# Another order of the 766 steps of a hand-scheduled attention and expert kernel

## Chip, core and metric

The kernel runs on one NeuronCore of a Trainium2 chip, as one launch. The metric is the device time of a launch in microseconds (us). The profile names the core's engines PE (TensorE, matmuls), PEld (its weight loads, which overlap matmuls), DVE (VectorE), ACT (ScalarE), POOL (GpSimd) and SP (SyncE, which here only issues transfers). PSUM, into which TensorE writes, has 8 banks of 128 x 512 float32.

## The reference

Two stages, with batch 4, sequence 768. The first is attention of 8 heads of 64 columns, in which each row sees its neighbours closer than 16 and one summary key and value of each of the 24 blocks of 32 rows. The second takes the 512 columns of the 8 heads as `x`, and runs 4 experts of causal attention with a head of 64, of which a gate picks 2 per row.

```python
k_sum = k.reshape(B, H, nb, block, D).max(axis=3)      # nb = 24, block = 32
v_sum = v.reshape(B, H, nb, block, D).mean(axis=3)
scores_l = scale * q @ k^T, masked to |i - j| < 16
scores_s = scale * q @ k_sum^T + log(block)
attn = softmax([scores_l, scores_s]) @ [v, v_sum]
...
logits = x @ w_gate                                     # 2 of 4 experts per row
for e in range(E):
    q, k, v = x @ wq[e], x @ wk[e], x @ wv[e]
    ye = softmax(causal(scale * q @ k^T)) @ v @ wo[e]
    out += w[e] * ye                                    # where e was picked
```

## The kernel before

The kernel has no scheduler at run time or at build time: `make_plan` lists 766 steps, each a few instructions with the buffers that it reads and writes, and `TABLE` (lines 55 to 108) is a text of 766 entries `step,engine,slots` that says in which order the steps are emitted, on which engine each runs (V VectorE, A ScalarE, G GpSimd, S SyncE, P TensorE), and which slots its new buffers take. `Plan.emit` walks the table; a semaphore is waited for wherever a step reads what another engine wrote, or overwrites a slot that another engine still reads. Each engine takes its own entries strictly in the table's order, so a step that waits holds up all later steps of its engine, transfers that this engine issues among them.

Steps have names. `b` is the batch (0 to 3), `c` the pair of heads (0 to 3), `g` the half of the heads, `cc` the pair of experts, `u` a block of scores (0 to 5):

- loads: `dk`, `dq` (keys and queries, issued by GpSimd, lines 261 and 266), `dv` b c (values, four transfers from SyncE into one of six `vb` slots, lines 284 to 287), `dw..`, `dwo`, `dwg` (weights), `dvs` (values by blocks of 32 into the one `vt` slot, line 339);
- set-up: `id16`, `id32`, `idr` (identities), `mt` (mask), `pi`, `kwz`, `knz` (three memsets of 4 x 1024 into the key slots, line 219), `sel` (the selector of block sums, lines 240 to 244), `vtz`, `v2o`, `vone` (ones in a `vb` slot, lines 210 to 214), `w1m` and `at` (a first exponential), `cvg`, `cg`, `cw0`, `cw1`, `co` (weights to half precision);
- block sums: for batches 0 and 1 by TensorE, `bs` (line 304), then `be` on VectorE (L170, L322) and `ds`, a copy into the `vb` slot; for batches 2 and 3 by GpSimd, `tr` (line 347) and `ds`. `hc` copies 32 rows of each window within the `vb` slot (L170, 32 x 1408);
- first stage, per b and c: `tk`, `tq` (transposes, L366), `kw`, `rk`, `ksc`, `cq` (key windows, block maxima and queries out of PSUM, and the copy of the key sums, L170, 128 x 288), `sc` (scores, L414 and L420), `ex` (exponentials, L427), `av` (L437), `rc`, `xm` (division, L448 and L452), `tx` (transposes, L463), `hi`, `lo` (two half-precision parts, L482);
- second stage, per b: `vp` (values and gate, L554 and L557), `lg`, `v2`, `ga`, `gx`, `gb`, `gc` (gate); per cc: `pp` and `pc` (projections, L630, and their copy to half precision), `sp` (scores, L654), `es` (exponentials, L662), `dm` (causal mask, L667, on GpSimd), `aw` (L678), `r2`, `wv` (L697 to L704), `tw` (L715), `ct`; then `op` (L737), `oc` (copy out of PSUM) and `od` (transfer to memory, L748);
- `fl0` to `fl23`: dummy matmuls on zeros (L769), four of 512 columns for the first eight and one for the others. With engine P they run; with engine A the entry emits nothing.

The digits behind a name are b, c or cc, and so on: `bs01` is the block sum of batch 0, pair 1; `pp310` a projection of batch 3, second pair of experts; `op34` the last piece of the output product. Lines such as L170 and L168 belong to a copy helper for all engines.

TensorE's array is used in different shapes: whole for `vp`, `pp`, `aw`, `op` and `fl`, in 64 rows for `sc`, `sp`, `tx`, `tw`, in 64 or 32 columns for `tk`, `tq`, `av`, `bs`.

Of the kernel before, what the change touches and what calls it, by code (L numbers as in the profile page):

```python
# [15 lines left out]
S = 768  # L16
# [42 lines left out]
95,A, 99,P,6.0.0 40,V,3 77,P,4.3 51,G, 234,S,3 68,P,0.0 78,A, 126,P,1.2 69,V, 80,A, 98,P, 243,G,0 127,A, 44,G, 70,A,  # L59
62,G, 122,P,4.2.2 236,S,4 100,V, 105,P,5.1.1 101,V, 82,P,2.1.1 148,G, 106,A, 81,P, 124,V, 102,P,0.0.0 83,V, 123,A,  # L60
125,G, 107,V, 109,P,6.0 233,G,2 103,A, 84,V, 45,G, 130,P,4.4 144,S,0 110,A, 104,V, 143,S, 269,P,7.0.0 131,A, 141,S,
235,G, 128,P,2.5 271,V, 63,P,6.1 129,A, 145,S,1 108,G, 133,P,0.0.2 270,A, 64,V, 140,S, 132,P, 142,S, 252,P,4.2.2
134,V, 111,P,2.0 135,V, 242,G,0 65,G, 254,V, 113,P,6.1 112,A, 237,G, 85,P,0.1.1 114,A, 86,V, 136,P,2.2.2 272,G, 137,A,
115,P,6.1.0 273,P,5.1 138,V, 150,G, 116,P, 274,A, 87,V, 46,V, 253,A, 238,P,2.0 117,V, 118,V, 246,S,5 277,P,0.2 239,V,
275,P,4.3 278,A, 119,P,6.3.3 256,P,3.2 276,A, 120,V, 241,G, 286,P,2.1.1 303,P,0.0.0 257,A, 194,P,4.0 121,V, 406,S,0
304,A, 244,S,2 255,G, 288,V, 149,G, 196,P,6.1 195,A, 305,V, 240,G, 287,A, 260,P,4.4 147,V, 407,S, 280,P,0.0.1 261,A,
409,S, 247,G, 290,P,3.0 197,A, 307,P,2.1 291,V, 279,P, 308,A, 204,P,4.0 402,S,4 281,V, 213,P,6 152,P,2.0.0 205,A,
282,V, 214,A, 245,G, 258,P,0.5 154,V, 283,P,4.4.4 259,A, 153,V, 408,S, 198,P,6 215,G, 201,P,2 284,V, 146,S, 199,A,
289,G, 248,P,0.1 418,S,0 306,G, 285,V, 401,G,1 202,A, 309,P,6.0 249,V, 210,P,4 310,A, 262,P,2.1.2 211,A, 263,P, 251,G,
165,P,0.2 250,A, 404,S,3 264,V, 265,V, 415,G,0 294,P,6.1 403,G, 166,A, 266,P,4.5.5 292,P,2.2 295,A, 267,V, 158,P,0  # L70
293,A, 400,G,0 151,A, 155,P,6 410,G, 159,V, 268,V, 160,A, 311,P,2.3 157,V, 207,P,4 312,A, 167,P,0.0 156,V, 161,V,6.0
208,A, 163,V, 411,G,0 314,P,2.0.0 162,A, 168,V, 432,P,7.2 313,P, 164,V, 433,A, 169,P,4.1 315,V, 172,P,0 170,A, 316,V,
413,G, 296,P,6.1.1 584,S,0 582,S, 585,S, 449,P,2.0 583,S, 173,A, 181,P,4 203,G, 450,V, 297,P, 412,G, 182,A, 184,P,0
178,P,2 416,S,2 298,V, 299,V, 185,A, 175,P,4 179,A, 209,G, 317,P,0.6.6 183,G, 300,P,6.7.7 174,G, 318,V, 176,A, 206,G,
428,P,2.2.2 200,G, 445,P,3.1.1 171,G, 319,V, 301,A, 177,G, 362,P,4.1 429,A, 414,G,2 447,V, 186,G, 180,G, 302,V,
364,P,0.0 448,A, 576,G,1 446,A, 430,V, 212,G, 586,G, 217,P,0.0.6 363,A, 218,P, 365,V, 431,A, 216,P, 375,P,2.0 219,V,
369,P,4 376,A, 187,P,1.1.0 220,V, 189,P, 587,G,1 370,A, 188,P, 434,P,2.5 190,V, 366,P,6 191,V, 323,P,4.1.1 367,A,
435,A, 436,P,0.4 417,G, 325,V, 420,S,0 453,P,6.3 423,S, 192,P,2.0 324,V, 454,A, 421,S, 320,P,4 193,V, 422,S, 368,G,
437,A, 578,S,5 405,G, 221,P,2.1 322,A, 372,P,6 222,V, 479,P,0.0.0 373,A, 419,G, 462,P,1.2.1 321,V, 381,P,2 223,P,4.0
464,V, 480,A, 577,G,2 335,P,6.2 382,A, 224,V, 463,A, 377,G, 383,G, 590,G,2 326,P,2 336,A, 481,V, 225,S, 371,G, 374,G,  # L80
378,P,4 327,V, 333,P,6.0 328,A, 329,V,1.1 424,G, 331,V, 330,A, 379,A, 229,P,2.2 332,V, 334,A, 451,P,4.0 230,V, 380,G,
226,P,0.4 452,A, 425,G,0 346,P,6.1 227,V, 343,P,4 347,A, 385,P,1.0.2 384,P, 386,P, 344,A, 228,S, 349,P,0 387,V,
# [819 lines left out]
```

## Time and profile before

| | us |
|---|---|
| median of 3 runs | 162.57 |
| lowest, highest | 161.71, 163.44 |
| profiled execution, its own time | 163.03 |
| its span (first to last instruction) | 161.3 |
| bytes read, written in it | 24.13 MB, 6.29 MB |

A profile is one execution of the program, recorded instruction by instruction. The span is shorter than the time by what lies before and behind. Busy time is the union of an engine's records; matmul records overlap, and each goes on some 0.2 us behind the point at which the next may start, so a short wait of TensorE can look shorter than it is. "Idle before" names what ended an idle stretch, read from the semaphores.

### The profile page before, as it was taken

What the parts mean: (1) busy time and instruction counts of PE and PEld (TensorE: products, weight loads), DVE (VectorE), ACT (ScalarE), POOL (GpSimd) and SP (SyncE); (2) the same over time, 40 slices, a digit from 0 to 9 for tenths busy, and PEclk for the clock granted to TensorE, in tenths of its full rate; (3) what the DMA queues carried; (4) which work ended last, traced back from release to release, by engine and by line L of the source; (5) the groups of instructions that cost most, each with busy time, mean ns of one, the idle gap of its engine ahead of it and who ended that gap; (6) DMA issues with size and microseconds to landing.
All of it is one profiled execution on the core that took longest, in us unless ns stands there. A gap on an engine that the chain in (4) does not pass through costs nothing.

```text
span 161.3 us, 6957 instructions
## 1 busy us (share of the span) xinstructions
PE 146.8 (91%) x2999; PEld 108.0 (67%) x2999; DVE 116.6 (72%) x241; ACT 117.9 (73%) x150; POOL 111.8 (69%) x181
## 2 busy tenths in 40 slices
PE   0249998899999999999999999999999998999997
PEld 0127796786776866688656979666778895476742
DVE  5675488989885577986877887847978578247770
ACT  3032499758998969988978795787867894999540
POOL 6899969777775999969999999629994340135100
DMA  3999999998699995993899749886000000030746
GB/s 27 210 220 212 205 179 227 209 219 163 154 176 207 228 207 135 171 201 53 201 219 221 216 107 161 191 291 254 24 0 4 4 4 0 6 130 0 257 167 230
DMA packets 44158, 24.57 MB, mean 152 GB/s; under 512 B 33120, under 2 KB 40544, under 8 KB 43744
## 3 DMA queue, kind: packets, MB, share of 16 engines
q1 hardware_dynamic: 35280, 16.52, 43.2%
q0 software_dynamic: 7488, 6.29, 26.2%
q10 hardware_dynamic: 1360, 1.32, 2.3%
q8 instruction: 23, 0.38, 1.0%
q14 instruction: 7, 0.06, 0.1%
HBM read 24.13 MB, written 6.29 MB: 189 GB/s over the span
## 4 chain that ended last, share of the span: by engine, by line
PE 65%; POOL 21%; issue 6%; ACT 4%; DVE 3%; POOLq 0%; DVEq 0%; ACTq 0%
PE ps L437 12%; PE ps L630 11%; POOL vb L170 7%; PE ps L554 6%; PE ps L678 6%; PE ps L304 4%; PE ps L366 4%; PE ps L654 4%; PE ps L737 3%; PE ps L463 3%; PE ps L414 3%; POOL vt L347 3%; PE ps L769 3%; POOL a L667 2%; PE ps L420 2%
## 5 line engine op out<-in xcount | busy, mean ns | idle before, releaser
L662 ACT ACTIVATE a<-ps 128x1024 f16<-128x1024 f32 (+1 forms) x48 | 41.8, 918 | 5.2 <-PE ps L654 4.8
L667 POOL TENSOR_SCALAR_AFFINE_SELECT a<-a 128x256 f16<-128x256 f16 x48 | 18.6, 406 | 21.0 <-ACT a L662 20.4
L427 ACT ACTIVATE aT<-ps 120x768 f32<-120x768 f32 x32 | 25.0, 816 | 9.2 <-PE ps L420 9.0
L437 PE MATMUL ps<-vb,aT 120*64 120x65 f32 x768 | 27.3, 224 | 1.2 <-issue 0.6
L437 PEld LDWEIGHTS ps<-vb,aT 120*64 120x64 f32 x768 | 24.4, 138 | 4.3 <-issue 2.1
L170 POOL COPY vb<-vb 32x1408 f32<-32x1408 f32 x16 | 21.9, 1373 | 2.9 <-DMA vb<-in_v_dram 2.1
L630 PE MATMUL ps<-hi,wqk 128*128 128x384 f16 x128 | 23.1, 326 | 0.7 <-ACT ob L168 0.3
L347 POOL TENSOR_TENSOR vt<-vt 120x1024 f32<-120x1024 f32 (+3 forms) x16 | 19.2, 1200 | 6.4 <-issue 4.1
L630 PEld LDWEIGHTS <-wqk 128*128 128x128 f16 x128 | 11.8, 98 | 9.6 <-issue 2.2
L382 DVE TENSOR_REDUCE ks<-ps 128x24 f16<-128x768 f16 x16 | 15.1, 951 | 3.7 <-PE ps L366 3.3
L482 DVE TENSOR_TENSOR lo<-ps,hi 128x768 f16<-128x768 f32 x16 | 15.1, 954 | 1.3 <-ACT hi L168 1.1
L452 DVE TENSOR_TENSOR x<-ps,rec 128x768 f32<-128x768 f32 x16 | 15.3, 956 | 0.5
L366 PE MATMUL ps<-idr,kn 100*64 100x100 f16 x256 | 8.5, 218 | 7.3 <-DMA kn<-in_k_dram 7.3
L654 PE MATMUL ps<-qk,qk 64*128 64x512 f16 (+3 forms) x128 | 14.4, 306 | 0.5 <-ACT qk L168 0.4
L554 PE MATMUL ps<-wvg,hi 128*128 128x264 f16 x96 | 13.8, 275 | 0.1
L170 POOL COPY vb<-vu 24x768 f32<-24x768 f32 x16 | 13.2, 822 | 0.8
L168 ACT COPY kw<-ps 128x1152 f16<-128x1152 f16 x12 | 13.5, 1133 | 0.0
L168 ACT COPY qT<-ps 128x768 f16<-128x768 f16 x12 | 9.5, 806 | 5.3 <-PE ps L366 5.2
L678 PE MATMUL ps<-v,a 128*128 128x65 f16 x336 | 12.3, 193 | 0.2
L366 PEld LDWEIGHTS <-kn 100*64 100x64 f16 x256 | 7.0, 116 | 8.1 <-DVE vb L210 5.7
L678 PEld LDWEIGHTS <-a 128*128 128x128 f16 x336 | 11.0, 97 | 2.1 <-issue 1.0
L737 PE MATMUL ps<-wo,wT 128*128 128x512 f16 (+1 forms) x50 | 11.9, 371 | 0.0
(95 smaller groups left out, 273.8 us busy)
## 6 DMA issues: line engine op xcount, KB each, us to landing
vb<-in_v_dram SPq DMA_DIRECT2D x32, 176.0 KB, 6.1
out_dram<-ob SPq DMA_DIRECT2D x9, 512.0 KB, 3.4
vt<-in_v_dram SPq DMA_DIRECT2D x16, 192.0 KB
kn<-in_k_dram POOLq DMA_DIRECT2D x6, 384.0 KB, 7.5
qn<-in_q_dram POOLq DMA_DIRECT2D x6, 384.0 KB, 7.4
out_dram<-ob ACTq DMA_DIRECT2D x2, 512.0 KB
kn<-in_k_dram POOLq DMA_DIRECT2D x4, 192.0 KB, 5.5
qn<-in_q_dram POOLq DMA_DIRECT2D x4, 192.0 KB, 5.5
```

Of the source, the lines that this page charges most:

```text
L168: nc.scalar.copy(dst, src)
L170: en(e).tensor_copy(dst, src)
L347: en(e).tensor_tensor(y[0:120], x[0:120, 0:w], x[0:120, w:2 * w], AL.add)
L366: nc.tensor.transpose(dst[64 * hp:64 * hp + 64, p * s:p * s + p], src[:, hh + hp, 64 * s:64 * s + 64], idt)
L427: nc.scalar.activation(T["aT"][aT.slot][0:KR], pbank(sc, 2)[0:KR, :, 0:384], AF.Exp, scale=SCALE)
L437: nc.tensor.matmul(pbank(av, 2)[o:o + 64, u, 65 * (2 * (t // 2) + hp):65 * (2 * (t // 2) + hp) + 65], a[0:KR, hp, 64 * t:64 * t + 64], T[" ...
L554: nc.tensor.matmul(p[:, i, 0:264], hi_(ch)[:, cols], T["wvg"][:, ch, :], start=(ch == 0), stop=False, skip_group_check=True)
L630: nc.tensor.matmul(pbank(pp, 2)[:, u, 0:384], T["wqk"][:, cc, ch, j, :], hi_(ch)[:, 384 * u:384 * u + 384], start=(ch == 0), stop=(ch == N ...
L654: nc.tensor.matmul(pbank(sp, 2)[:, ep, c0:c0 + w], T["qk"][qk[1].slot][r, 128 * tj:128 * tj + 128], T["qk"][qk[0].slot][r, n0:n0 + w], sta ...
L662: nc.scalar.activation(a2v(u), pbank(sp, 2)[:, :, 0:ln], AF.Exp, scale=SCALE / (XS * XS))
L667: nc.gpsimd.affine_select(m, m, [[0, 2], [1, 128]], AL.is_ge, 0.0, base=0, channel_multiplier=-1)
L678: nc.tensor.matmul(pbank(av, 2)[:, ep, 65 * ti:65 * ti + 65], a2v(u)[:, ep, o:o + 128], T["v2"][v2.slot][:, tj, 2 * cc + ep, :], start=(tj ...
```

## The change

The diff touches nothing but `TABLE`. All 766 steps, their instructions and their buffers are the same; the order, the slots, and the engine of 73 steps differ. The first three and the last three lines of the two tables:

```diff
-2,G,0 139,A, 41,V,4 6,G, 8,V, 52,S,4 4,G, 7,G, 37,G,0 42,V,5 0,G, 5,G,0 47,S,0 1,A, 36,G, 3,G, 39,V,2 66,S,2 35,G,
-34,V, 59,G,1 58,G,1 71,P,0.0.0 43,G, 88,P,1.1.1 53,G, 90,V, 61,S,5 60,G, 54,P,2.0 72,V, 91,A, 89,A, 48,G, 73,V,
-92,P,3.0 55,V, 57,G, 75,P,4.1 93,A, 232,G,0 49,P,5.1 76,V, 74,A, 56,G, 96,P,6.0 50,V, 94,P,0.1 97,A, 79,P,2.2 67,G,
...
-742,P, 746,V, 754,P,4.4 747,V, 714,V, 748,V, 751,P,6.2 755,A, 715,V, 749,P,2 23,P,0 752,V, 756,A, 716,P,4 31,P,1
-717,A, 32,P,0 17,A,1 30,P,1 750,V, 753,A, 757,P,4.6 763,P,5.0 758,A, 760,P,0.1 27,P,1 764,V, 21,P,6 11,A,7 26,A,2
-761,V, 25,A,3 19,P,2 759,S, 765,A, 13,P,7 762,A, 15,A,4 28,A,1 16,A,3 18,A,5 14,P,6 33,P,2 10,P,0
+40,V,3 4,G,0 39,V,2 52,S,3 2,G, 6,G, 5,G,0 139,A, 3,G, 7,V, 35,G, 57,G,1 8,G, 47,S,2 59,G, 53,A, 71,P,0.0.0 42,V,5
+37,V,0 88,P,1.1.1 34,V, 43,G, 66,S,5 58,G,1 73,V, 36,G, 54,P,2.0 90,V, 0,V, 75,P,3.0 74,A, 89,A, 92,P,4.1 41,V,4
+61,S,4 93,A, 48,G, 60,G, 91,G, 49,P,5.1 72,V, 55,V, 94,P,6.0 76,A, 56,A, 95,A, 96,P,0.1 232,G,2 67,G, 77,P,2.2 50,V,
...
+15,A,2 714,V, 575,S, 751,P,6.0 715,V, 716,P,2 717,V, 747,V, 754,P,0.4 748,V, 752,A, 17,A,2 749,P,2 19,A,6 32,P,6
+753,A, 755,V, 750,A, 757,P,7.6 760,P,6.2 26,P,4 763,P,5.3 761,A, 11,P,4 13,P,2 758,V, 31,A,3 764,V, 27,P,0 756,S,
+24,A,1 18,A,7 10,P,1 765,S, 16,P,6 759,A, 762,A, 28,A,5 21,P,4 30,P,5 20,A,7 23,A,7 14,A,7 25,P,7
```

Read by engine, with names, the parts that the text below speaks of:

```
GpSimd before  dk000 id16 dk001 idr vone0 w1m dq001 mt dq000 kwz dk011 dq010 sel hc01 dq011 hc00
               dk010 dk100 ds01 hc03 ds00 dq110 id32 hc02 cg ksc03 dq100 vtz hc10 ksc02 dk110 ds02
               hc11 ksc11 cw1 ds11 ksc10 cw0 ds10 hc13 hc12 dm015 ksc12 ksc13 dq200 ds13 ...
GpSimd after   dk001 dk000 id16 dq001 dq000 kwz dk010 knz dk011 sel dq010 mt hc00 dq011 ksc01 dk100
               hc03 ds00 dq110 hc02 id32 vtz dq100 ds03 ksc02 dk110 ds02 ksc10 hc11 cw1 hc23 ds10
               ds11 ksc13 co cvg hc13 hc12 cg cw0 dq200 v2o ds12 ...
SyncE before   dv01 dv00 dv03 dv02 dv10 dv11 dw11 dw10 dw01 dwv1 dw00 dwv0 dv13 dvs200 dv12 dvs201
               dvs203 dv20 dvs202 dwo dv23 ...
SyncE after    dv01 dv00 dv03 dv02 dv10 dv11 dw10 dw11 dv23 dv13 dwo dwv0 dwv1 dv12 dvs200 dw01 dw00
               dvs203 dvs201 dvs202 dv30 dv20 ...
TensorE before tk00 tk01 bs01 tq01 tq00 bs00 sc011 sc010 sc001 av011 sc000 bs03 tq03 av010 tk03 ...
TensorE after  tk00 tk01 bs01 tq00 tq01 bs00 sc010 sc011 sc000 tk03 bs03 sc001 tk02 av011 av010 ...
TensorE before ... op22 aw300 aw301 sp311 aw311 aw310 fl19 tw300 aw302 tw310 aw312 op31 op30 tw311
(its end)      fl13 tw301 fl21 fl22 fl20 op32 op34 op33 fl17 fl11 fl9 fl3 fl4 fl23 fl0
TensorE after  ... sp311 aw301 aw300 op21 aw310 aw311 op22 tw300 aw302 tw310 aw312 op30 tw301 op31
(its end)      tw311 fl22 op32 op33 fl16 op34 fl1 fl3 fl17 fl0 fl6 fl11 fl20 fl15
```

Of the 73 steps that change their engine, these go from GpSimd to ACT: `hc01`, `ds01`, `ksc03`, `hc10`, `ksc12`, `ds13`, `ksc22`, `ksc30` to `ksc33`; from ACT to GpSimd: `ksc01`, `ds03`, `ds12`, `co`, `ksc20`, `ksc21`; from DVE to GpSimd: `knz`, `v2o`, `cvg`; from GpSimd to DVE: `idr`, `vone0`, `w1m`, `ksc11`. 18 copies out of PSUM go from DVE to ACT and 18 others from ACT to DVE; three output transfers change between ACT's and SyncE's queues. The dummy matmuls that run number 22 instead of 21.

More of the change, by code (lines that the diff above doesn't have):

```diff
@@ L61 @@
[L61 to L70, printed above, removed]
@@ new lines @@
+142,S, 145,S, 117,V, 244,S,4 273,P,1.0 235,A, 238,P,6.0 137,A, 256,P,7.2 274,A, 406,S,0 118,V, 270,A, 138,V, 257,A,
+119,P,2.3.3 141,S, 150,G, 275,P,4.2 276,A, 239,V, 277,P,0.3 140,S, 419,G, 278,A, 120,V, 121,V, 303,P,6.1.0 286,P,7.2.2
+288,V, 194,P,4.0 195,V, 304,A, 240,G, 289,A, 290,P,0.1 287,A, 307,P,1.0 258,P,2.4 305,V, 291,V, 241,G, 259,A, 308,A,
+306,G, 151,G, 196,P,4.1 147,G, 247,G, 245,G, 197,V, 260,P,6.5 292,P,2.0 261,A, 309,P,0.1 310,A, 409,S, 198,P,4.1
+293,A, 407,S, 279,P,6.0.1 280,P, 148,G, 281,V, 199,A, 311,P,0.2 312,A, 204,P,2 205,A, 282,V, 149,G, 401,G,0
@@ new lines @@
+263,P,4.1.2 46,G, 408,S, 283,P,6.4.4 284,A, 207,P,0 285,V, 578,S,3 248,P,2.1 208,A, 249,V, 250,G, 400,G,2 201,P,0
+210,P,6 262,P, 206,G, 410,G, 264,V, 265,V, 152,P,2.0.0 153,V, 411,G,0 202,A, 211,A, 402,S,0 167,P,0.2 168,V, 154,A,
+266,P,6.5.5 267,V, 251,A, 585,S,0 213,P,2 165,P,4.0 214,A, 268,V, 158,P,0 294,P,2.3 200,G, 166,A, 159,V, 169,P,4.0
+295,A, 203,G, 170,A, 582,S, 155,P,6 160,V, 584,S, 156,V, 157,V, 172,P,0 181,P,2 583,S, 314,P,4.0.0 173,A, 174,G,
+161,V,6.0 313,P, 215,G, 163,V, 315,V, 182,A, 162,A, 184,P,0 449,P,7.2 296,P,2.1.1 212,G, 316,V, 297,P, 183,G, 209,G,
@@ new lines @@
+178,P,4 185,A, 164,V, 404,S,4 298,V, 299,V, 175,P,0 171,G, 450,A, 179,A, 413,G, 216,P,0.0.6 176,A, 180,G, 218,P,
+217,P, 414,G,0 219,V, 220,V, 576,G,1 432,P,2.0 317,P,4.6.6 433,A, 318,V, 300,P,0.7.7 301,A, 302,V, 428,P,3.0.1
+445,P,2.1.2 362,P,6.1 186,G, 429,A, 177,G, 586,G, 364,P,0.0 319,V, 587,G,1 363,V, 430,V, 446,A, 189,P,1.1.4 365,A,
+369,P,6.1 370,A, 431,G, 422,S,0 366,P,0 447,V, 367,A, 405,G, 188,P, 187,P, 190,V, 375,P,2 376,A, 421,S, 403,G, 448,G,
+323,P,6.1.1 191,V, 324,V, 325,A, 221,P,0.0 436,P,4.5 423,S, 462,P,2.2.0 377,G, 368,G, 192,P,6.1 222,V, 193,V, 371,G,
@@ new lines @@
+438,P,0.0.0 439,P, 349,P,2 341,A, 457,V, 458,V, 440,V, 441,V, 342,G, 427,G, 348,G, 487,P,4.3 608,P,6.2 609,V,
+621,P,7.1.2 350,A, 351,G, 488,A, 339,G, 389,P,0.0 390,V, 485,P,2.0 486,A, 623,V, 468,P,4.2 469,A, 604,P,6.0.0 606,V,
+352,P,0 459,P,2.0.0 605,V, 345,G, 353,A, 354,G, 470,P,4.1 356,P,1.1.0 355,P, 357,P, 228,S, 624,A, 591,G,1 471,A,
+460,A, 489,P,4.1.1 358,V, 359,V, 461,V, 625,P,6.1 490,P, 426,G, 360,P,0.1 361,V, 9,G, 622,A, 592,S,5 626,A, 607,A,
+629,P,6.4 442,P,2.1.1 630,A, 491,V, 443,A, 492,V, 444,V, 473,P,0.0.2 627,P,6.5 612,P,4.0 628,A, 613,A, 472,P, 474,V,
@@ L108 @@
+569,S, 739,G, 573,P,2.2 736,G, 743,V, 571,A, 712,P,6.0 713,A, 574,A, 744,V, 572,S, 709,P, 745,P,6.1 746,V, 742,P,
+15,A,2 714,V, 575,S, 751,P,6.0 715,V, 716,P,2 717,V, 747,V, 754,P,0.4 748,V, 752,A, 17,A,2 749,P,2 19,A,6 32,P,6
+753,A, 755,V, 750,A, 757,P,7.6 760,P,6.2 26,P,4 763,P,5.3 761,A, 11,P,4 13,P,2 758,V, 31,A,3 764,V, 27,P,0 756,S,
+24,A,1 18,A,7 10,P,1 765,S, 16,P,6 759,A, 762,A, 28,A,5 21,P,4 30,P,5 20,A,7 23,A,7 14,A,7 25,P,7
 """
```

61 lines of the change are left out of this document (25 added, 36 removed).

## The prediction

> **What bounds the kernel now.** I read the page first, then the busy time by stage, then the timelines of TensorE and GpSimd. The page gives engine, busy time and share, and the chain of waits by engine:
>
> ```profile
> span 161.3 us, 6957 instructions
> PE 146.8 (91%) x2999; PEld 108.0 (67%) x2999; DVE 116.6 (72%) x241; ACT 117.9 (73%) x150; POOL 111.8 (69%) x181
> DMA  3999999998699995993899749886000000030746
> PE 65%; POOL 21%; issue 6%; ACT 4%; DVE 3%; POOLq 0%; DVEq 0%; ACTq 0%
> ```
>
> TensorE is the bound, GpSimd the second link of the chain, and the DMA engines are full for most of the first 70 us. The busy time by stage (columns: stretch, its length, then busy time and instructions of PE, weight loads, DVE, ACT, POOL, then clock, DMA share, GB/s) says where TensorE still stands idle:
>
> ```profile
> 0.00:18.25 18.25, 8.72 (x146) 6.25 (x146) 11.58 (x35) 5.23 (x8) 16.05 (x41) 1.00 1.03 174
> 18.25:38.00 19.75, 18.32 (x582) 16.12 (x578) 16.22 (x33) 15.84 (x20) 15.16 (x20) 1.00 1.14 203
> 38.00:75.00 37.00, 35.98 (x743) 26.72 (x738) 29.08 (x53) 32.09 (x40) 30.96 (x41) 1.00 0.95 177
> 75.00:98.00 23.00, 22.64 (x501) 16.69 (x499) 17.57 (x35) 20.04 (x27) 22.04 (x33) 1.00 0.84 177
> 98.00:134.00 36.00, 35.89 (x769) 27.55 (x766) 27.77 (x51) 27.56 (x35) 22.91 (x38) 1.00 0.36 99
> 134.00:152.00 18.00, 17.11 (x228) 10.89 (x227) 10.55 (x28) 15.13 (x19) 4.64 (x12) 1.00 0.20 73
> 152.00:161.30 9.30, 8.19 (x64) 3.78 (x60) 3.88 (x11) 1.97 (x3) 0.00 (x0) 1.00 0.54 201
> ```
>
> Length less PE: 9.5, 1.4, 1.0, 0.4, 0.1, 0.9, 1.1. TensorE's work is the same in both orders, so another order can win only from these 14.4 us, of which 9.5 lie before 18.25 us, and 98 to 134 us offers nothing. The change moves almost every step but alters no operation, so I take it by the four places where an order can show: the shape changes, the head, GpSimd's queue in the middle, the end.
>
> **Shape changes.** Rows of TensorE's timeline (start, duration of the records, line):
>
> ```profile
> 77.87 1.04 PE L737 MATMUL ps<-wo,wT 128*128 128x512 f16 x4
> 78.75 1.46 PE L630 MATMUL ps<-hi,wqk 128*128 128x384 f16 x8
> 82.86 1.03 PE L737 MATMUL ps<-wo,wT 128*128 128x512 f16 x4
> 83.82 0.34 PE L414 MATMUL ps<-pi,mt 64*128 64x384 f16 x2
> ```
>
> The same four matmuls cost 0.88 us when a full-array step follows (78.75 - 77.87) and 0.96 when a 64-row step does (83.82 - 82.86): a change costs about 0.08 to 0.10. With three classes (full array: `pp`, `vp`, `aw`, `op`, `fl`; 64 rows: `sc`, `sp`, `tx`, `tw`; 64 or 32 columns: `tk`, `tq`, `av`, `bs`) I count 111 changes in the table before and 112 after. That is **+0.1 us**.
>
> **The head.** First TensorE, then GpSimd in order of time, then groups (busy us, mean ns of one):
>
> ```profile
> 10.52 0.63 PE L304 MATMUL ps<-vb,sel 96*32 96x128 f32 x2 [1.42 <-POOL sel L244]
> 11.92 1.50 PE L304 MATMUL ps<-vb,sel 96*32 96x128 f32 x22 [0.78 <-POOL vb L170]
> 14.78 1.51 PE L304 MATMUL ps<-vb,sel 96*32 96x128 f32 x24
> 19.59 0.87 PE L304 MATMUL ps<-vb,sel 96*32 96x128 f32 x24
> ```
> ```profile
> 3.36 0.51 POOL L225 COPY idr<-id 100x2 f16<-100x2 f16 x3
> 4.85 0.72 POOL L266 DMA_DIRECT2D qn<-in_q_dram  x1
> 5.57 0.22 POOL L195 MEMSET mt<- 128x128 f16 x1
> 7.16 0.72 POOL L266 DMA_DIRECT2D qn<-in_q_dram  x1
> 9.63 0.17 POOL L240 MEMSET sel<- 96x56 f32 x1
> 12.54 1.37 POOL L170 COPY vb<-vb 32x1408 f32<-32x1408 f32 x1
> ```
> ```profile
> L170 POOL COPY vb<-vb 32x1408 f32<-32x1408 f32 x16 | 21.9, 1373 | 2.9 <-DMA vb<-in_v_dram 2.1
> L170 POOL COPY vb<-vs 24x1536 f32<-24x1536 f32 x6 | 8.8, 1465 | 3.5 <-DVE vs L322 3.3
> L261 POOL DMA_DIRECT2D kn<-in_k_dram x10 | 6.8, 683 | 1.9 <-PE ps L366 1.1 <-POOLq L886 0.8
> L170 POOL COPY kw<-ks 128x288 f16<-128x288 f16 x12 | 4.9, 421 | 1.1 <-DVE ks L382 0.8
> L170 POOL CAST wqk<-a 128x512 f16<-128x512 f32 x4 | 2.3, 606 | 0.0
> L250 POOL MEMSET vt<- 128x2048 f32 x1 | 1.8, 1823 | 0.0
> L757 ACT ACT_TABLE_LOAD x1 | 1.3, 1283 | 1.3 <-PEq L886 1.3
> ```
>
> TensorE waits for GpSimd here: `bs01` begins at 10.52 when `sel` is made and goes on at 11.92 when the edge copy `hc01` is; `bs00` follows at 14.78. The change puts `knz` on GpSimd: three memsets of 1024 elements, each half of the vt row, 0.91 to 1.0 us, 2.9 in all. Ahead of `sel` it adds `knz` 2.9 and one more key issue 0.68, and takes away `idr`, `vone0` and `w1m` (4.85 - 3.36 = 1.5), `mt` (7.16 - 5.57 = 1.6) and one query issue 0.72: -0.2, so `sel` is ready near 10.3. Up to `hc00` the same 2.9 and 0.68 come in, and 1.5, `hc01` 1.37 and one query issue 0.72 go: 0.0, so `hc00` ends at 13.9 as before (12.54 + 1.37). `hc01` is now ACT's, behind the load of ACT's table (1.28 us, which the built order puts in front of it): about 10.5. So `bs01` runs from 10.5 in one piece, 1.2 us earlier, but TensorE then stands until `hc00` frees `bs00` near 14.1 instead of 14.78. Behind that, `hc10` (1.37) leaves the queue ahead of `ds02`, while `ds03` takes the place of `ds01`; what the attention of batch 0 waits for comes up to 2 us sooner. ACT takes part of it back, as it holds `hc01`, `ds01` and `hc10` now, each 1.4 us. I take **-0.6 us** by 38 us (bounds -2.0 and, for the clock below, +1.7): 0.7 shows at `bs00`, and TensorE's idle time from 18.25 to 38 is only 1.4.
>
> **GpSimd in the middle.** In the chain GpSimd leads from 75 to 96 us, where TensorE takes over:
>
> ```profile
> 94.95 1.13 POOL a L667 x3
> 96.13 1.39 PE ps L678 x40
> ```
>
> The masks at L667 release `aw100`. GpSimd is idle for 12.8 us of the first 75 (75 less 16.05, 15.16 and 30.96) and for only 1.0 of the next 23: there TensorE is in step with GpSimd's queue. Ahead of the last of these masks the new queue holds in addition `knz` 2.9, `co` and `cvg` 2.4 (four halves of 0.606), `ds03` and `ds12` 2.9 and three key-sum copies 1.3; it has lost `hc01` and `hc10` 2.7, `ds01` and `ds13` 2.9, five key-sum copies 2.1 and the 1.5 of `idr`, `vone0` and `w1m`. That is 9.5 against 9.2: **the queue is as long as before, and the masks hang on its idle time**. Laying the new queue out with these prices I find, as estimates, waits of 0.9 for `be02`, 1.3 for `rk10` and 1.7 for `rk13` beside the starting 1.4 and some 1.5 of small gaps: 6.8. To this comes `cw0`, whose weights `dw01` and `dw00` are now issued after `dv23`, `dv13`, `dwo` and `dv12`: 1 to 3 us; and `tr300` may wait 0 to 2 for its rows. Idle time of 8 to 12 us instead of 12.8 lets the masks end 0.5 to 4.5 us earlier. TensorE can use no more of it than the 1.4 us that it lacks between 38 and 98, and some waits are new. I take **-0.7 us** (bounds -1.4 and +2).
>
> **The end.** Rows of ACT's timeline and of its groups, of the chain, and of ACT's DMA queue:
>
> ```profile
> 135.78 0.80 ACT L168 CAST qk<-ps 128x768 f16<-128x768 f32 x1 [0.45 <-PE ps L630]
> 143.74 2.85 ACT L662 ACTIVATE a<-ps 128x1024 f16<-128x1024 f32 x3 [0.37 <-PE ps L654]
> 146.76 1.30 ACT L662 ACTIVATE a<-ps 128x256 f16<-128x256 f32 x2 [0.16 <-PE ps L654]
> ```
> ```profile
> L168 ACT CAST v<-ps 128x512 f16<-128x512 f32 x4 | 2.4, 594 | 0.6 <-DVE lgp L563 0.6
> ```
> ```profile
> 156.74 3.45 PE ps L769 x16
> ```
> ```profile
> 157.06 0.85 ACTq L748 DMA_DIRECT2D out_dram<-ob  x2
> ```
>
> From the end of `pc300` (before: 135.78 + 0.80) ACT now runs ten long exponentials (2.85 / 3 = 0.95 each), two short ones (1.30 - 0.95 = 0.35), `pc310` 0.80 and `v231` 0.6, before `es311` is out: 11.6 us, and about 12.5 with two waits for TensorE. TensorE's own steps of that stretch come to some 11.3, an estimate from their spacing before; then `aw310` wants the very banks that `es311` reads, whereas before it took others. So `aw310` is some 1.2 us late, where the whole stretch from 134 to 152 lost 0.9 and, as I read it, 0.5 of that here. I take **+0.7** (0 to +1.3).
>
> Behind the last output matmul stood 16 dummy matmuls, 3.45 us, 0.216 each; they end at 160.2, 1.1 before the span does. After the change 20 stand behind `op34` and one between `op33` and `op34`, where before the spare ones sat in a wait. Five more at the end are 5 x 0.216 = **+1.0** (rounded down, bounds +0.2 and +1.1). The low bound is the case that the last transfers, issued at 157.06 to 157.91, already set the end together with the dummies and move with `op34` alone. They are issued about as late as before, and I find nothing else that would end behind the dummies.
>
> **The sum.** 161.3 + 0.1 - 0.6 - 0.7 + 0.7 + 1.0 = 161.8. Around the span lay 1.7 us (163.03 - 161.3): 163.5. The profiled execution was 0.46 above the median of its three runs (162.57), so a median of the changed kernel should lie a little lower: **163.3 us**, 0.4% above. A difference under 1% (1.6 us) can't be told from none here, as the three runs of before span 1.7 us.
>
> **Rivals.** First, *GpSimd in step, later*. By my terms TensorE reaches the masks' first reader, now `aw101`, 1.3 us earlier than `aw100` before and with 0.4 us more of its work ahead of it: 96.1 - 1.3 + 0.4 = 95.2. The masks end at 96.1 + 0.3 less what GpSimd's idle time falls short of 12.8, so from 11.6 us of idle time on they decide; my waits at their upper ends give 11.8, and each further wait counts in full. With 2 us that I don't see it is 13.8, the masks end at 97.4, and the time is 163.3 + 2.2 = 165.5. For it: DMA digits of mostly 9 until 70 us, and two full `v` loads put ahead of the weights. Against it: four copies of 1.4 us went to ACT and only two came back, and ACT is idle for 4.9 us between 38 and 75.
>
> [...]
>
> Second, *half speed for longer*: the same 24 matmuls took 1.51 us at 14.78 and 0.87 at 19.59, though the clock column says 1.00: until about 18 us TensorE runs at half pace, after 6 us without a gap (from 11.92). The new head has a gap of some 0.8 us before `bs00` at 14.1. If the pace turns only after a full stretch without a gap, it turns up to 3.4 us later (18.25 less 14.78, the one unbroken stretch that I can date) and costs half of it: +1.7, 165.0. Against it: a gap of 0.8 may not count, and part of that time TensorE waits for others anyway.
>
> [...]
>
> Third, *the head pays in full*: the 2.0 of the bound instead of 0.6, and the 1.4 between 38 and 98 instead of 0.7, is 161.2; with the end's ACT term at 0.3 it is 160.8. For it: `hc10` and `hc01` leave the engine that TensorE waits for, and nothing in the new order between 38 and 98 asks GpSimd for more. Against it: ACT's three copies, and that every wait of this order would have to be hidden.
>
> That the change is no change can't be: the dummies alone move the end.
>
> **Chances.** Forecast (161.0 to 164.2) 0.42; GpSimd in step 0.26; half speed 0.12; head in full 0.20. So faster by over 1% 0.20, within 1% 0.42, slower 0.38. Leaving out a tenth at each end, the range goes to 160.6 below (just under the third rival) and to 166.4 above (inside the first).
>
> **What would show it.** In the profile after: `bs01` near 10.6 in one piece, `bs00` at 14.1 to 14.5; the shift from 1.51 to 0.87 us of a block sum at `bs03` near 18; GpSimd's idle time before 75 us (12.8 now); a wait of `cw0` on DMA; `aw310` waiting for ACT L662; a last stretch of 20 dummy matmuls of 4.3 us and no output transfer behind it. If the dummies end before the last transfer lands, the fourth term is wrong; if `aw101` follows the masks without a gap at 96 us or later, the first rival is right; if TensorE has lost several us anywhere between 98 and 134 us, none of this holds.

## The result and the profile after

The changed kernel takes 167.0 us (median of 17 runs, 163.79 to 170.85); the kernel before, in as many runs, 162.57 (161.71 to 164.55). The ratio is 1.0155 (95% interval 1.0121 to 1.0188): slower by 1.5%. That ratio leaves out the runs that lie over 1.5% above the fastest of their kernel, 11 of the changed kernel's 17 and the profiled one among them; the medians of all runs stand at 1.027. The changed kernel's times are spread over 7 us and those of before over 3.

The profiled execution took 168.35 us, its span is 166.6. Its page gives engine, busy time and the chain of waits by engine:

```profile
span 166.6 us, 6958 instructions
PE 146.7 (88%) x3000; PEld 107.6 (65%) x3000; DVE 114.4 (69%) x245; ACT 121.4 (73%) x155; POOL 110.2 (66%) x172
...
PE 58%; DMA 11%; POOL 10%; ACT 7%; issue 6%; DVE 4%; SPq 2%; POOLq 0%; DVEq 0%; ACTq 0%
```

TensorE's work is the same, and transfers now hold 11% of the chain, where the chain of before had no share for them. The busy time by stage, in the stretches of the prediction (length, then PE, weight loads, DVE, ACT, POOL, clock, DMA share, GB/s):

```profile
0.00:18.25 18.25, 6.99 (x134) 5.34 (x136) 9.38 (x40) 5.93 (x7) 15.06 (x33) 1.00 1.06 176
18.25:38.00 19.75, 16.25 (x490) 13.92 (x486) 15.01 (x28) 16.34 (x21) 13.36 (x15) 1.00 1.00 163
38.00:75.00 37.00, 35.78 (x778) 27.01 (x771) 26.82 (x51) 29.93 (x38) 28.82 (x40) 1.00 0.97 178
75.00:98.00 23.00, 21.50 (x446) 15.69 (x444) 15.09 (x34) 19.00 (x25) 21.90 (x31) 1.00 0.75 156
98.00:134.00 36.00, 35.75 (x791) 27.01 (x787) 29.67 (x51) 30.04 (x42) 25.24 (x40) 1.00 0.57 132
134.00:152.00 18.00, 17.07 (x254) 11.61 (x249) 10.47 (x18) 14.23 (x19) 3.87 (x11) 1.00 0.08 31
152.00:166.70 14.70, 13.38 (x152) 7.05 (x152) 7.98 (x27) 5.90 (x9) 1.94 (x6) 1.00 0.48 179
```

Length less PE is 11.3, 3.5, 1.2, 1.5, 0.3, 0.9, 1.3. Against the kernel before that is +1.7 in the head, +2.1 up to 38 us and +1.1 between 75 and 98, with little elsewhere. What TensorE waited for (engine, line, releaser: us in total, times, the longest):

```profile
PE ps L304 <- DMA vb<-in_v_dram: 2.6, 1, 2.6
PE ps L304 <- ACT vb L168: 1.8, 1, 1.8
PE ps L420 <- POOL kw L170: 1.5, 1, 1.5
PE ps L437 <- issue: 1.3, 1, 1.3
...
PE ps L304 <- issue: 0.9, 1, 0.9
```

Three things stand here that the kernel before did not have in this size. `bs01` waits 1.8 us for ACT's `hc01` (before: 0.8, for the same copy on GpSimd). A first-stage score (L420, `sc201`) waits for a key-sum copy on GpSimd, `ksc20`. And twice TensorE stops for "issue", which means that nothing in the profile released it; such stops of the kernel before are of 0.3 us at most. The places, in TensorE's timeline:

```profile
11.04 0.61 PE L304 MATMUL ps<-vb,sel 96*32 96x128 f32 x2 [2.57 <-DMA vb<-in_v_dram]
13.42 1.50 PE L304 MATMUL ps<-vb,sel 96*32 96x128 f32 x22 [1.77 <-ACT vb L168]
...
16.27 1.33 PE L304 MATMUL ps<-vb,sel 96*32 96x128 f32 x24
...
30.77 0.33 PE L437 MATMUL ps<-vb,aT 120*64 120x65 f32 x2
32.44 3.01 PE L437 MATMUL ps<-vb,aT 120*64 120x65 f32 x94 [1.34 <-issue]
...
36.35 0.43 PE L304 MATMUL ps<-vb,sel 96*32 96x128 f32 x8
37.68 1.31 PE L304 MATMUL ps<-vb,sel 96*32 96x128 f32 x40 [0.90 <-issue]
```

The two stops for issue lie inside a step: `av030` stands behind its second matmul record, `bs10` behind its eighth. (The expectations below call the first place `av031`; by the table that is the step behind it.) The profile shows no semaphore that is waited for there. From one instruction to the next they take 1.6 and 1.2 us. On ACT, ahead of `hc01`:

```profile
10.71 1.28 ACT L168 ACT_TABLE_LOAD   x1 [10.71 <-DMA vb<-in_v_dram]
12.00 1.36 ACT L168 COPY vb<-vb 32x1408 f32<-32x1408 f32 x1
```

And on GpSimd, from the wait of `hc23` (39.14) over `cw0` (54.55) to `tr300` and `ksc20`, the copy that `sc201` waits for (the profile puts the wait of `hc23` down to `bs10`, which ended just then but shares no buffer with it; the rows that `hc23` copies, `dv23`, landed at 39.0 to 39.2):

```profile
39.14 1.35 POOL L170 COPY vb<-vb 32x1408 f32<-32x1408 f32 x1 [3.40 <-PE ps L304]
...
54.55 1.17 POOL L170 CAST wqk<-a 128x512 f16<-128x512 f32 x2 [1.79 <-DMA a<-in_moe_wq_dram]
...
73.08 5.04 POOL L347 TENSOR_TENSOR vt<-vt 120x1024 f32<-120x1024 f32 x4 [1.03 <-DMA vt<-in_v_dram]
...
78.45 0.42 POOL L170 COPY kw<-ks 128x288 f16<-128x288 f16 x1
```

GpSimd's idle time before 75 us is 75 less 15.06, 13.36 and 28.82: 17.8, where it was 12.8.

### The profile page after: what moved, and what is told of

It reads as the page before. It is cut to its first block, busy times and chain, and to the rows that moved or that the text cites. A ratio compares the mean times of both kernels' runs of the same rounds, so it can differ in the third digit from the quotient of the medians.

```text
span 166.6 us, 6958 instructions
## 1 busy us (share of the span) xinstructions
PE 146.7 (88%) x3000; PEld 107.6 (65%) x3000; DVE 114.4 (69%) x245; ACT 121.4 (73%) x155; POOL 110.2 (66%) x172
## 4 chain that ended last, share of the span: by engine, by line
PE 58%; DMA 11%; POOL 10%; ACT 7%; issue 6%; DVE 4%; SPq 2%; POOLq 0%; DVEq 0%; ACTq 0%
PE ps L437 10%; PE ps L630 9%; DMA vb<-in_v_dram 7%; PE ps L737 6%; POOL vt L347 6%; PE ps L678 5%; PE ps L366 5%; PE ps L554 5%; DMA vt<-in_v_dram 4%; PE ps L654 4%; PE ps L769 3%; PE ps L463 3%; PE ps L414 3%; ACT aT L427 2%; PE ps L420 2%
## 5 line engine op out<-in xcount | busy, mean ns | idle before, releaser
L437 PE MATMUL ps<-vb,aT 120*64 120x65 f32 x768 | 26.5, 224 | 2.3 <-issue 1.3
L667 POOL TENSOR_SCALAR_AFFINE_SELECT a<-a 128x256 f16<-128x256 f16 x48 | 18.1, 405 | 15.5 <-ACT a L662 15.0
L437 PEld LDWEIGHTS ps<-vb,aT 120*64 120x64 f32 x768 | 24.1, 138 | 4.9 <-issue 2.5
L347 POOL TENSOR_TENSOR vt<-vt 120x1024 f32<-120x1024 f32 (+3 forms) x16 | 19.2, 1200 | 10.5 <-DMA vt<-in_v_dram 9.7
L630 PE MATMUL ps<-hi,wqk 128*128 128x384 f16 x128 | 23.2, 326 | 0.2
L170 POOL COPY vb<-vb 32x1408 f32<-32x1408 f32 x14 | 18.7, 1350 | 5.0 <-PE ps L304 3.4
L654 PE MATMUL ps<-qk,qk 64*128 64x512 f16 (+3 forms) x128 | 14.1, 306 | 1.0 <-ACT qk L168 0.7
L304 PE MATMUL ps<-vb,sel 96*32 96x128 f32 x192 | 8.5, 307 | 5.3 <-DMA vb<-in_v_dram 2.6
L737 PE MATMUL ps<-wo,wT 128*128 128x512 f16 (+1 forms) x50 | 12.5, 371 | 0.0
L168 ACT CAST hi<-ps 128x768 f16<-128x768 f32 x11 | 8.8, 797 | 5.0 <-PE ps L463 4.9
```

The source lines that it names most:

```text
L170: en(e).tensor_copy(dst, src)
L347: en(e).tensor_tensor(y[0:120], x[0:120, 0:w], x[0:120, w:2 * w], AL.add)
L437: nc.tensor.matmul(pbank(av, 2)[o:o + 64, u, 65 * (2 * (t // 2) + hp):65 * (2 * (t // 2) + hp) + 65], a[0:KR, hp, 64 * t:64 * t + 64], T[" ...
L630: nc.tensor.matmul(pbank(pp, 2)[:, u, 0:384], T["wqk"][:, cc, ch, j, :], hi_(ch)[:, 384 * u:384 * u + 384], start=(ch == 0), stop=(ch == N ...
L654: nc.tensor.matmul(pbank(sp, 2)[:, ep, c0:c0 + w], T["qk"][qk[1].slot][r, 128 * tj:128 * tj + 128], T["qk"][qk[0].slot][r, n0:n0 + w], sta ...
L667: nc.gpsimd.affine_select(m, m, [[0, 2], [1, 128]], AL.is_ge, 0.0, base=0, channel_multiplier=-1)
```

## The experiments

All are edits of the table, on the changed kernel unless said otherwise. Each was timed beside the kernel before on the same chip, in 6 runs (the last in 12). In the first four, line numbers are 3 higher than in the other profiles (L437 is L440 there).

### The changed kernel again

> The changed kernel unaltered, profiled a second time. Theory A (the loss is in the order itself): the same stalls at the same steps, bs01 cut in two with 1.5 to 2 us between its parts, a wait of sc220 for the key-sum copy on GpSimd near 79 us of about 1.5 us, and a time 1.5 to 3% above the kernel before. Theory B (much of the loss is the moment at which transfers and code arrive, which differs between runs): the two breaks of 1.3 and 0.9 us in the middle of av031 and bs10, for which the profile names no releaser, are gone or sit elsewhere, and the span differs by 1 us or more from the 166.6 us of the first profile.

(The step named sc220 there is `sc201`.) Measured: 167.81 us, before 163.01; ratio 1.0299 (1.0235 to 1.0362). The head is other than in the first profile: the rows of `dv01` came earlier, `bs01` was cut in two again, with 1.1 us idle, and `bs00` started at 14.92. In `av030` is the same stop, now longer, at the very same instruction:

```profile
29.64 0.33 PE L440 MATMUL ps<-vb,aT 120*64 120x65 f32 x2
32.30 4.58 PE L440 MATMUL ps<-vb,aT 120*64 120x65 f32 x94 [2.33 <-issue]
```

The 94 matmuls behind it take 4.58 us, against 3.01 in the first profile. The busy time by stretches of 2 us says why (the three last columns are clock, DMA share, GB/s):

```profile
30.00:32.00 2.00, 0.00 (x0) 0.00 (x0) 1.05 (x2) 1.98 (x4) 1.85 (x2) 1.00 0.83 126
32.00:34.00 2.00, 1.70 (x32) 1.70 (x34) 0.00 (x0) 0.86 (x1) 1.91 (x3) 0.58 0.94 159
34.00:36.00 2.00, 2.00 (x46) 2.00 (x45) 0.76 (x2) 0.00 (x0) 0.60 (x2) 0.57 0.00 0
```

Behind the stop TensorE's clock is granted at 0.58 and 0.57, and the DMA engines run dry (0.00), since the next loads (`dv23` first, issued at 35.20) wait for slots that `av030`, `av031` and their followers free. The stop in `bs10` is gone. The wait for the key-sum copy, 1.5 us by theory A, is short in this profile:

```profile
PE ps L423 <- POOL kw L173: 0.3, 1, 0.3
```

So neither theory holds as written. The time and the cut in `bs01` are those of A, the short wait is not; of B's signs the stop in `bs10` is gone, but the one in `av030` stays at its place and the span is the same (166.7 against 166.6). What differs between executions is the length of the stop and what follows it.

### The head

```diff
+0,V, 1,A, (at the front of the table)
-0,V,      (behind 90,V,)
-1,A,      (behind 102,P,)
```

> Only w1m and at (the small first exponential, before which ACT's table of functions is loaded) go back to the front of the table, where the kernel before has them in effect. Theory A, head: the table load leaves the path of hc01, which then starts when its rows have landed, near 10.7 instead of 12.0; bs01 ends 1.3 us earlier, bs00 starts near 15.0 instead of 16.3 (held then by hc00, which ended at 14.6), and the time falls by 1.0 to 1.4 us against the changed kernel. Rival: GpSimd and the transfers set the pace behind the head, and the time falls by less than 0.4 us although bs00 is earlier.

Measured: 168.44 us (1.0318, 1.0250 to 1.0387), no gain, where theory A had 1.0 to 1.4. The load left the path as expected (it ran at 0.80 us), and what was late next is in TensorE's rows of this run:

```profile
11.52 1.50 PE L307 MATMUL ps<-vb,sel 96*32 96x128 f32 x22 [0.60 <-ACT vb L171]
12.96 1.49 PE L369 MATMUL ps<-id,qn 128*64 128x128 f16 x24
14.51 0.63 PE L307 MATMUL ps<-vb,sel 96*32 96x128 f32 x2
15.81 1.50 PE L307 MATMUL ps<-vb,sel 96*32 96x128 f32 x22 [0.67 <-POOL vb L173]
```

`bs01` goes on at 11.52 instead of 12.07, but `bs00` breaks for `hc00`, and in this execution TensorE stayed at half pace until 21.5 us (the 24 matmuls of a block sum took 1.51 us at 20.08; in the run before 0.86 at 18.97). The head was not what the time hung on here.

### GpSimd's queue

Four edits: `hc23` later; two key-sum copies back on ACT; both; the transfers of `cw0`'s weights earlier.

```diff
-419,G, (behind 140,S,)   +419,G, (behind 149,G,)
-431,G, 448,G,            +431,A, 448,A,
-141,S, 140,S,            +141,S, 140,S, (behind 144,S,)
```

> Only hc23, a copy for batch 2 that waits 3.4 us on GpSimd at 36 us for transfers dv23, moves back behind cw0 in the table. If GpSimd's queue as a whole is in step with TensorE (theory A, middle): GpSimd's idle time before 75 us falls from 17.8 by about 2, ksc20 comes earlier, TensorE's wait of 1.5 us near 79 shrinks below 0.5, and the time falls by 0.8 to 1.5 us. Rival: be10 and the weights' transfers hold the queue anyway (waits of 1.7, 1.5 and 1.8 us follow within 15 us), tr300 still starts with the landing of its rows near 73, and the time stays within 0.4 us.

> Only ksc20 and ksc21, two key-sum copies of 0.42 us that the change put on GpSimd behind tr301, go back to ACT. Theory A, middle: TensorE's wait of 1.5 us near 79 us goes, nothing else is late behind it, and the time falls by 1.2 to 1.5 us. Rival: the masks or hc20 and hc21 on GpSimd are late next, some 0.5 us is gained, or none.

> hc23 behind cw0 and ksc20, ksc21 on ACT, both edits of the two runs before. If TensorE is held twice, by late code in av031 near 30 us and by GpSimd's queue near 79 us, and either alone hides the other: with the second taken away by the copies on ACT, an execution without the break in av031 (TensorE 3 us earlier at 38 us) can keep its lead: 163 to 164.5 us, and an execution with the break gives 166. Rival: the break in av031 is not a cause of time, since GpSimd's rows (tr300, hc20) hold TensorE behind 79 us in any case: 166 us with or without the break, and waits of TensorE on GpSimd of 1 us or more between 75 and 100 us.

> Only dw01 and dw00 move: on SyncE's queue they are issued right behind dw11, ahead of dv23, dv13, dwo, dwv0, dwv1, dv12 and dvs200 (the order of the kernel before). Theory A, middle (rival 1 of the prediction): cw0 no longer waits (1.4 to 2.4 us in four profiles), GpSimd's queue from cw0 to ksc20, which holds no further wait, comes forward by as much, TensorE's wait for ksc20 near 79 us shrinks by 1.4 us or goes, and the time falls by 1.0 to 1.8 us. Rival: the transfers that it pushes back (dv23, dv13) make hc23 and hc13 wait longer, cw0 starts no earlier than before, and the time stays within 0.5 us or rises.

Measured: `hc23` late 168.81 us (1.0350, 1.0285 to 1.0415), no gain; the copies on ACT 166.04 (1.0167, 1.0094 to 1.0239), 1.8 less than the changed kernel on the same chip, with intervals that just touch; both 168.25 (1.0281, 1.0209 to 1.0352); the weights early 166.45 (1.0185, 1.0124 to 1.0246). The last two ran on a chip on which the unaltered changed kernel was not timed.

The copies on ACT did what theory A asks: TensorE's wait at L420 is gone from the profile, and the span is 165.4 although `av030` stops for 2.5 us in it. TensorE's place in the profiles, by its instructions counted from the start (matmuls and weight loads; 2500 lies ahead of `sc201`, 2874 is where `sc201` goes on behind its wait), shows what held it:

```
profile            at 2500  at 2874  at 3200  at 5900
changed            67.50    78.93    89.00    156.54
changed, again     68.79    79.02    89.09    156.56
exponential first  68.22    78.97    89.04    156.76
hc23 late          65.46    77.20    88.82    156.11
copies on ACT      67.50    77.15    87.99    155.28
dq100 late         66.32    76.76    86.84    154.30
```

In the first three TensorE came to `sc201` at different times and went on at the same one: there `ksc20` on GpSimd held it. With the copies on ACT it came as early as in the first profile, went on 1.8 us earlier and kept 1.3 of it to the end. (The last row is of a run further below.) The run with `hc23` late shows the other side. Its profile has no stop in `av030`, and TensorE was 2 us earlier at 75 us than in the first profile; there it met GpSimd's queue:

```profile
75.15 0.33 PE L417 MATMUL ps<-pi,mt 64*128 64x384 f16 x2
77.20 0.35 PE L423 MATMUL ps<-qT,kw 64*128 64x64 f16 x12 [1.72 <-POOL kw L173]
```
```profile
78.00:80.00 2.00, 2.00 (x50) 1.43 (x48) 1.58 (x3) 1.22 (x2) 1.94 (x3) 0.65 0.75 198
80.00:82.00 2.00, 2.00 (x8) 0.81 (x7) 1.97 (x2) 1.94 (x2) 2.00 (x5) 0.50 0.99 193
```

The wait is about the old one (1.72), the clock falls to 0.50 behind it, of a lead of 2 us 0.2 is left at instruction 3200, and the span is 166.2. So in this execution the copy on GpSimd and the half clock cost what the missing stop had saved. The run with both edits was meant to show whether either alone hides the other, and its profile does not settle it: there TensorE stopped for 1.7 us in `bs10` instead and waited 1.0 us for a mask, as the rival had it, and the span is 165.8.

Moving `hc23` cannot have taken away the stop of `av030`, which ends at 32.44 in the first profile, before GpSimd comes to `hc23` (35.7). Whether the stop comes differs between executions.

With the weights early, `cw0` does not wait any more, yet starts at 55.8, no earlier than in the two profiles of the changed kernel (54.5 and 55.6), as `hc23` ahead of it now waits 5.6 us. That is the rival's sign. The median of 166.45 says little beside the profile's span of 169.9 us; the run is inconclusive on time.

### The end

```diff
-11,P,4 13,P,2 27,P,0 10,P,1 16,P,6 21,P,4 30,P,5 25,P,7
+11,A,4 13,A,2 27,A,0 10,A,1 16,A,6 21,A,4 30,A,5 25,A,7
```

The second run does the same to 27, 21, 19, 13, 14, 33 and 10 in the kernel before.

> The changed kernel without the 20 dummy matmuls behind op34; no result depends on them. By the prediction's fourth term the end falls by 4.3 us to the landing of the last transfer. The profile has that landing at 164.95 and the end of the dummies at 165.67: 0.7 us is gained, no more. Rival: the dummies keep something fast that the last transfers need, and nothing or less is gained.

> The kernel before without the 16 dummy matmuls behind its last output matmul. Its last transfer lands at 160.28, its dummies end at 160.19: no difference (within 0.3 us) against the kernel before. Together with the run before this one: if the changed kernel gains 0.7 and the one before nothing, the prediction's +1.0 for the end was +0.7; if both gain alike, the dummies were no term of the difference.

Measured: 166.97 us for the changed kernel (1.0212, 1.0145 to 1.0279), 163.79 for the one before (1.0029, 0.9970 to 1.0088; 163.83 unedited on that chip). The second is no difference, as expected. For the first the spread hides 0.7 us, but its profile shows it: from the last output matmul at 159.60 to the end of the span at 164.6 are 5.0 us. In the changed kernel:

```profile
160.97 0.38 PE L737 MATMUL ps<-wo,wT 128*128 128x256 f16 x2
161.19 4.48 PE L769 MATMUL ps<-zz 128*128 128x512 f16 x20
```

160.97 to 166.64 are 5.7: the dummies cost some 0.7. In the kernel before they cost nothing, as the last transfer lands when they end (160.28 against 160.19).

### The stop in av030

The trace lists the packets of each DMA queue. Those of q8, which the page lists as instructions (23 packets, 0.38 MB), are blocks of 16384 bytes. Matmuls and weight loads counted from the start, the stops come at 705, 961 and 1217, which is 256 apart; 23 blocks of 256 are 5888, which fits TensorE's 6000. For the third block in each profile: when its packet ran, how many instructions TensorE had begun by then, and when TensorE stood at 961 (from the start of the instruction before to that of 961).

```
profile            packet          begun  stood at 961
before             26.75 to 28.03  779    no
before, no tail    26.25 to 27.28  775    no
changed            30.16 to 31.14  907    30.88 to 32.44
changed, again     29.77 to 30.99  961    29.75 to 32.30
exponential first  30.97 to 32.16  927    31.55 to 33.61
hc23 late          25.61 to 26.73  765    no
copies on ACT      29.36 to 30.57  961    29.35 to 31.87
both               27.97 to 28.93  870    29.79 to 30.25
weights early      30.48 to 31.52  961    30.32 to 32.94
no tail            29.50 to 30.78  907    30.25 to 32.05
```

TensorE goes on 1.3 to 1.45 us after the block has landed, in each of the seven. In the three profiles without the stop it starts at instruction 765 to 779; that point, near 770, is taken here as the one at which it is due. Two runs ask whether a transfer stands in front of it, and which, and two combine:

```diff
-143,S,0 144,S,  +143,S,0 144,S, (behind 418,S,5: dw10 and dw11 behind dv23)
-233,G,2         +233,G,2        (behind 108,G,: dq100 behind ksc02)
```

> Only dw10 and dw11, two transfers of 256 KB that SyncE issues near 24.5 to 26.5 us, move behind dv23 on its queue, some 8 us later. TensorE's code comes in blocks of 16 KB through the DMA engines; the third block's transfer began 2.4 to 4.3 us late in seven of the eight profiles of this order, and TensorE stood at the block's first instruction (in or just before av031). Theory C (these two transfers stand in front of it): the third block's transfer begins within 0.8 us of its usual point, the break of 1.3 to 2.6 us at av031 is gone, TensorE is 2 to 3 us earlier at 34 us, and no half clock follows. Rival: other transfers (dv11, dq100) stand in front, the block is late by 2 us or more and the break stays. The time by itself says little, since cw1, and with it pp010, may come later: 165 to 169 us in either case.

> The same move, with ksc20 and ksc21 on ACT and without the 20 dummy matmuls at the end. If the loss of this order is the sum of the late code (with the half clock behind it), GpSimd's queue before 79 us and the dummies: all three gone gives 161.5 to 164 us, as fast as the kernel before (ratio 0.99 to 1.01). Rival: the waits only move (GpSimd's masks and rows are late next, or cw1), and it stays at 165 to 167 us (ratio 1.015 or more).

> Only dq100, a transfer of queries that GpSimd issues near 24.5 us, moves behind ds03 and ksc02 on GpSimd's queue, to about 26.5 us, behind the point near 26 us at which TensorE's third block of code is due. In the profiles with a late block its transfer began 0.2 to 1.7 us behind the first landing of dq100's pieces. Theory D (dq100 stands in front of the block): the third block begins within 1 us of its due point, the break at av031 is gone, TensorE is 2 us or more earlier at 34 us, and the median falls to 164 to 166 us. Rival (it is not one transfer, but how much is under way, and chance): the third block is late by 2 us or more, or the second or the fourth is instead, and the median stays at 167 us or above (ratio 1.025 or more).

> The same move with ksc20 and ksc21 on ACT and without the 20 dummy matmuls at the end: a second profile for the question of the run before, and the sum of what can be taken back in single edits. By theory D 162 to 164 us (ratio 0.995 to 1.01): 1.3 for the two copies and 0.7 for the dummies below the run before. By its rival 165 us or more (ratio 1.015 or more).

Measured: `dw10` and `dw11` late 169.57 us (1.0236, 1.0158 to 1.0315), with the packet at 30.45 and the stop from 30.22 to 32.86: theory C fell. With the copies and without the tail 168.62 (1.0326, 1.0259 to 1.0394): here the second block was late (27.17), TensorE stood at 705 for 2.3 us, and `cw1`, now late too, held `pp010`.

`dq100` late: 166.71 us (1.0129, 1.0040 to 1.0218; runs from 164.06 to 169.91). The packet ran at 25.84, and `av030` has no stop:

```profile
29.72 1.62 PE L437 MATMUL ps<-vb,aT 120*64 120x65 f32 x48
31.55 1.62 PE L437 MATMUL ps<-vb,aT 120*64 120x65 f32 x48 [0.21 <-POOL vb L170]
```

With the copies on ACT and no tail: 163.81 us (12 runs, 162.44 to 170.04), before 163.41; ratio 1.0032 (0.9984 to 1.0079). The third block ran at 27.25 and stopped nothing; the fourth was late and cost 1.6 us at 1217. TensorE's waits between 60 and 102 us in that run are these, and GpSimd is not among them:

```profile
PE ps L715 <- ACT v L168: 0.3, 1, 0.3
PE ps L366 <- ACT a L662: 0.2, 1, 0.2
PE ps L654 <- ACT qk L168: 0.2, 1, 0.2
```

So one transfer two places later on GpSimd, two copies on another engine and 20 dummies fewer take the loss back (ratio 1.0032, against 1.0155 and 1.0299 unaltered); the result is no faster than the kernel before. Alone, the move of `dq100` gives a median inside the changed kernel's own spread. That it brings the third block in time rests on two profiles of two, against two of the ten with the order's own place of `dq100`, and the fourth block was late in one of them. Against theory D stands the kernel before: it issues `dq100` at 24.5 and 24.0 us in its two profiles, 2.1 us ahead of instruction 770, as the changed order does (24.78, also 2.1 ahead), and its third block is in time. So theory D is open. What is shown is that a late block stops TensorE (0.5 to 2.6 us in the seven profiles above). Spans of single profiles side by side, with the two limits on and off:

| third block | copies on GpSimd | copies on ACT |
|---|---|---|
| late, `av030` stops | 166.6, 166.7 | 165.4 |
| in time | 166.2 (`hc23` late), 164.4 (`dq100` late) | 162.9 (no tail, which is worth 0.7) |

With the copies on ACT TensorE is 2.0 us ahead at instruction 961 when the third block is in time (29.83 against 31.87) and still 1.8 ahead at 5900 (153.48 against 155.28), although the fourth block was late in that run. With the copies on GpSimd the lead was lost in one profile (`hc23` late, behind the half clock) and in the other kept, 2.7 us at 961 and 2.2 at 5900 (`dq100` late against the first profile). So a late third block costs some 2 us, but not in every execution.

## Why the prediction failed where it did

The forecast's point was 163.3; the measured ratio puts the changed kernel near 165.1, and the median of all runs is 167.0. The range holds the first of these; the likeliest case, no change that can be told, was wrong, and the price of the first rival (165.5) was the nearest. That the range holds it is in part luck: the terms for the head and for GpSimd had the wrong sign, both terms of the end were too large, and a cost that no term had, late code, made up the difference.

**The shape changes, +0.1.** Not tested; nothing in the profile contradicts it.

**The head, -0.6: failed.** `sel` was ready at 10.2 as worked out (10.3). The step that failed is "about 10.5" for `hc01`: the prediction put it behind the table load, but left no room for that load behind the rows (in the profile of before they landed at 8.7 to 8.9; with 1.28 and 1.37 that is 11.4 or later). The load stands in front of ACT's first instruction and began only when the rows that this instruction copies had landed (10.63, the load at 10.71; in the second profile 9.29 and 9.36), 1.28 us on the path. The kernel before loaded at 1.27 us, for `at` stood first on ACT; the change moved `at` behind, which the prediction missed. With the last two transfers of `dv01` landing at 10.6 and 10.9 instead of 8.7 and 8.9, `bs00` began at 16.27, not 14.1. The run with the exponential first took the load away and won 0.5 at `bs01`, but nothing in the time; `hc00` was next, as the prediction had it.

**GpSimd in the middle, -0.7: failed.** The queue was as long as reckoned (with the idle time as it came, 17.8, the forecast puts the end of the masks at 96.1 + 0.3 + 5.0 = 101.4, and they ended at 101.2), but "idle time of 8 to 12 us" became 17.8, through waits that the prediction had not laid out: `dk110` for TensorE (2.8), `hc23` for the rows of `dv23` (3.4), `cvg` (1.5), besides `ksc13` (1.7) and `cw0` (1.8), which it had named. Two of them hang on TensorE's own delay: `dk110` waits for its transposes, and `dv23` could be issued only at 34.08, behind `av030`, its stop and `av031`. GpSimd ran without a gap from `tr300` to `ksc20`. The first rival named the mechanism; its victim was not the masks' reader but `sc201`, behind a copy that the change put on GpSimd, and the run with the copies on ACT shows what that is worth: 1.3 us at the end against the first profile, in which TensorE came to `sc201` as early, and 1.8 between medians.

**What no term had.** TensorE's code. The prediction treated every stop as a wait between engines; in the profile of before the blocks came in time, so no row pointed at it. In the first profile the two stops (1.3 and 0.9 us) are about the 2.1 us that the stretch up to 38 us lost. Where the third block is late, `av030` stops for 0.5 to 2.6 us, and where the clock fell behind it (0.58 and 0.57 in the second profile), its 94 matmuls took 1.6 us more (4.58 against 3.01).

**The end, +0.7 and +1.0: one wrong, one too large.** From the start of `pp301` to the last output matmul the kernel before took 23.4 us (132.99 to 156.35), the changed one 23.2 (137.75 to 160.97): the stretch as a whole is no longer, so ACT's exponentials cost nothing that shows. `es311` ended at 153.6, and `aw310` ran at 153.68, held 0.15 us; the 0.3 that TensorE did wait is at `aw301`, for a copy of the values on VectorE. The dummies cost some 0.7, since the last transfer lands only 0.7 ahead of their end; the bounds, +0.2 to +1.1, held it.

**Half speed for longer.** In the head the rival has no clear price: the turn to full pace came between 16 and 22 us in the twelve profiles of this order and its edits, but it differs within one order too; in the two profiles of the kernel before it came between 18.0 and 19.1 and between 15.7 and 16.2. That the pace turns only after a stretch without a gap, on which the 3.4 us of its price rest, was the author's estimate, and no run shows it. What the runs do show of half speed stands at another place, behind TensorE's stops (a granted clock of 0.58 and 0.57 in the second profile).

## What to carry to other kernels

When the steps were reordered here, the late arrival of TensorE's next block of code cost some 2 us where it cost time, and the wait for the copies on GpSimd 1.3; look in the packets for late instruction blocks wherever an engine stops inside a step for "issue". Two limits near the same moment can hide each other, as in the run with `hc23` late: an edit that takes one away and gains nothing has not shown that it was none. Comparing the time at which TensorE reaches the same instruction in each profile tells where a lead is won and lost. And ACT's table load (1.28 us) stood in front of ACT's first instruction: at 10.71 and 9.36 us where that was `hc01`, and off the path, at 1.27 and 0.80, where it was the small `at`.

## What the runs showed of the hardware

A late code block was not expected. Ten of the twelve profiles of this order and its edits have a stop of 1.6 to 2.6 us at a block's first instruction, the two of the kernel before none above 1.0. Full DMA engines alone are not the cause: from 26 to 30 us their share is 1.14 and 1.29 in the profile of before and 1.10 and 1.29 in the second profile of the changed kernel. Why the packet starts up to 4 us late in one execution and at once in another, with the same transfers issued within 0.6 us (the changed kernel again, and `hc23` late), stays open, and with it what in the new order makes it late.

From 20 to 95 us the clock, read by stretches of 2 us, was granted at 0.50 to 0.67 for 3 to 4 us behind each stop of 2.5 us or more (four cases: the changed kernel again, the copies on ACT, the weights early, `dw10` and `dw11` late), and behind three of 1.7 to 2.1 us (`hc23` late, both edits, and the weights early near 52 us, where it lasted for more than 6), but not behind others of 1.8 to 2.3 (no tail, exponential first, and the 2.3 us at 705 with `dw10` and `dw11` late, the copies and no tail). So the length of a stop did not decide it alone; what else did was not shown.
